# Order of the first loads, and of the work behind them, in a fused state-space and feed-forward kernel

## The chip, the cores and the metric

The kernel runs on one core of one Trainium2 chip. The metric is the device time in microseconds (us). The kernel before takes 155.22 us, the median of three runs; its profiled execution has a span of 152.3 us.

TensorE multiplies matrices and writes the results to the eight banks of PSUM. VectorE, ScalarE and GpSimd do the other arithmetic. Loads are issued from the queues of SyncE and of ScalarE and run on 16 DMA engines that all queues share.

## The reference

For an input x of 2048 rows and 448 columns, two results are computed and mixed row by row with a gate. One is a diagonal complex recurrence (a state-space layer), the other a feed-forward layer:

```python
g  = sigmoid((x * gate_w).sum(-1, keepdims=True))

dt      = exp(log_dt)
Lam_bar = exp(dt * Lam)                       # Lam complex, 448 values
B_bar   = ((Lam_bar - 1.0) / Lam)[:, None] * Bmat
Bu      = einsum("bld,pd->blp", x + 0j, B_bar)
for t in range(L):
    h = Lam_bar[None, :] * h + Bu[:, t, :]
y  = 2.0 * einsum("blp,dp->bld", hseq, Cmat).real + x * Dskip

b  = silu(x @ w1) @ w2                        # w1: 448 x 1792, w2: 1792 x 448
out = g * y + (1 - g) * b
```

## The kernel before

Rows of x are taken in pairs: 1024 pairs, "even" and "odd" rows. The recurrence is run over pairs, so it has 1024 steps; its input is B applied to the odd row plus B scaled by `Lam_bar` applied to the even row. Complex rotation is taken out with tables of sines and cosines, so that the recurrence becomes a real scan on VectorE.

The kernel keeps a list of operations for each engine in program order, and puts a semaphore wait ahead of an operation where it reads or writes what another engine or a load has still to finish. An operation can be several matmuls; its waits stand before the first of them. Within an engine the order of the program is the order of execution.

The loads at the head (`ld` is a plain load, `ldt` a transposing load on SyncE's queue; the first argument of `ld` is the queue that issues):

```python
        for i in range(4):                     # first half of even x, untransposed
            T.dma("act" if i % 2 else "sp", lambda e, i=i: e.dma_start(XH[:, i, :], x0[:, i, :]), writes=COK[i:i + 1])
        ld_w("sp", 0)                          # W1, rows 0 to 127, columns 0 to 767
        for i, (eng, v) in enumerate((("sp", A_log_dt), ("sp", A_Lambda_re), ("act", A_Lambda_im), ("act", A_Dskip))):
            ld(eng, R[i:i + 1, 0:D], row(v), f"R{i}", gR if i < 2 else gR2)
        ld_w("act", 1)
        ld_w("sp", 2)
        ld("act", W1E[0:64, 3, :], B_w1[384:448, :], "W1Ea")
        ld("act", W1E[64:128, 3, :], B_w1[384:448, :], "W1Ez")
        ld("sp", W1E[:, 0:3, FA:], B_w1[0:384, FA:]..., "W1Ed")          # W1, the other columns
        T.op("act", lambda e: e.activation(JK[:, 0, 0:1], HP[:, :], AF.Exp), ...)
        ld("sp", BB[:, 0:6:2, D:], A_B_re[0:384, :]..., "Bre", gB)
        ld("sp", BB[:, 1:6:2, D:], A_B_im[0:384, :]..., "Bim", gB)
        ldt(XT[:, 0:4, 512:1024], x2[512:1024, 0:512], "XTe1")           # second half of even x
        ...                                    # four small loads: B's last 64 rows, into Y3
        for h in range(2):                     # odd x
            ldt(XT[:, 4:7, h * 512:(h + 1) * 512], x2[h * 512:(h + 1) * 512, 512:896], f"XTo{h}")
```

The start of the computation: the first half of even x is transposed on TensorE and copied to SBUF; the first feed-forward pass over six blocks of 128 columns of W1 runs row block by row block; after its first row block (the `yield`) four tiny matmuls turn the parameter rows `R` into columns in PSUM bank 7, from where `PV` is copied.

```python
        for j in range(4):
            T.op("dve", lambda e, j=j: e.tensor_copy(XT[:, j, 0:512], xp[j]), ...)
        T.op("dve", lambda e: e.tensor_copy(XR[64:128, 0:512], xp[3][0:64, :]), reads=["ps7"], writes=["XR0a"])
        T.op("dve", lambda e: e.tensor_copy(XR[0:64, 0:512], xp[3][64:128, :]), reads=["ps7"], writes=["XR0b"])
        rd()                                   # VectorE: copies 64 columns inside R
        first = ffn1_first()
        next(first)
        T.op("pe", mm_cols, reads=["R0", "R1", "R2", "R3", "Rd", "ID"], writes=["ps7"])
        first = next(first)
        T.op("dve", ...)                       # PV <- bank 7
        ...                                    # some 30 tiny operations on PV: dt, mag, sn, cs, lr, li, ...

        def ffn1_first():
            banks = [nxt() for _ in range(NFA)]
            for j in range(4):
                for fb, bank in enumerate(banks):
                    T.op("pe", ... one matmul ..., reads=[f"W1Ej{j}" if j < 3 else "W1Ea", f"XTe0{j}"], ...)
                if j == 0:
                    yield
            yield list(enumerate(banks))
```

Every later feed-forward pass takes up to four column blocks at once: `whole()` has the three full row blocks, one operation for each column block; `rest()` has the last 64 rows, which run in pairs on the two halves of the array (XR holds those rows in the other half of the partitions), and is one operation for all four:

```python
            def rest():
                def mm(pe):
                    for i, (fb, bank) in enumerate(zip(fbs, banks)):
                        up = (i % 2 == 1) != bool(odd)
                        ...
                        ins = pe.matmul(ps[:, bank, :], W[p, jr, fb * 128:(fb + 1) * 128], x,
                                        start=rest_first, stop=not rest_first)
                    return ins
                T.op("pe", mm, ..., writes=[f"ps{bank}" for bank in banks])
```

Each bank is read by a Silu on ScalarE, which frees it. VectorE then works out phases for the tables (`phases(pt)`, three operations on 1024 elements for each of the four groups of 128 states) and the scaled B (`step_B(pt)`), each tile of which is transposed by a load into `LT` for the input projection on TensorE (`bu`):

```python
        step_B(0)
        phases(0)
        step_B(3)          # needs B's last 64 rows in Y3
        step_B(1)
        phases(3)
        step_B(2)
        phases(1)
        phases(2)
```

On TensorE there follow the rest of the feed-forward pass over the first half of even x, the pass over its second half, the input projection, the second feed-forward products, the same for odd x, the products `k0`, and the output tiles. On VectorE there follow the 16 gate sums, the scans, the scaling of C, and the mixing.

Of the kernel before, what the change touches and what calls it, by code (L numbers as in the profile page):

```python
# [19 lines left out]
D = 448  # L20
# [126 lines left out]
def gated_mix(nc, A_x, A_Lambda_re, A_Lambda_im, A_B_re, A_B_im, A_C_re, A_C_im, A_log_dt,  # L147
              A_Dskip, B_x, B_w1, B_w2, gate_w, out):
    with ExitStack() as ctx:
        E = ctx.enter_context  # L150
        T = Tracker(nc, ctx)

        def sb(name, shape, dtype):
            return E(nc.sbuf_tensor(name, list(shape), dtype))
# [4 lines left out]
        XT = sb("XT", [128, 7, NK], BF16)  # L159
# [3 lines left out]
        BB = sb("BB", [128, 7, 2 * D], BF16)  # L163
# [9 lines left out]
        XR = sb("XR", [128, NK], BF16)  # L173
# [29 lines left out]
        ps = E(nc.psum_tensor("ps", [128, 8, 512], F32))  # L203
# [3 lines left out]
        def ld(eng, dst, src, key, group=None):  # L207
            return T.dma(eng, lambda e: e.dma_start(dst, src), writes=[key], group=group)  # L208
# [18 lines left out]
        gR, gR2, gB = T.group(), T.group(), T.group()  # L227
# [19 lines left out]
        ld("act", W1E[0:64, 3, :], B_w1[384:448, :], "W1Ea")  # L247
        ld("act", W1E[64:128, 3, :], B_w1[384:448, :], "W1Ez")
        ld("sp", W1E[:, 0:3, FA:], B_w1[0:384, FA:].rearrange("(j p) f -> p j f", p=128), "W1Ed")
        T.op("act", lambda e: e.activation(JK[:, 0, 0:1], HP[:, :], AF.Exp), reads=["HP"], writes=["JK0"])  # L250
        ld("sp", BB[:, 0:6:2, D:], A_B_re[0:384, :].rearrange("(t p) d -> p t d", p=128), "Bre", gB)
        ld("sp", BB[:, 1:6:2, D:], A_B_im[0:384, :].rearrange("(t p) d -> p t d", p=128), "Bim", gB)
# [5 lines left out]
        for h in range(2):  # L258
# [11 lines left out]
             writes=["IOTA"])  # L270
# [9 lines left out]
        def nxt():  # L280
            n_bank[0] += 1
            return BANKS[(n_bank[0] - 1) % len(BANKS)]

        def ffn1_mm(c, fbs, rest_first):


            odd, h = c // 2, c % 2
            hs = slice(h * 512, (h + 1) * 512)
            W, w0, x0, jr = (W1O, 1, 4, 0) if odd else (W1E, 0, 0, 3)
            banks = [nxt() for _ in fbs]  # L290
            xk = XE[h] + [f"XTo{h}"] if odd else XE[h]

            def whole():
                for fb, bank in zip(fbs, banks):
                    def mm(pe, fb=fb, bank=bank):
                        ins = None
                        for j in range(3):
                            ins = pe.matmul(ps[:, bank, :], W[:, w0 + j, fb * 128:(fb + 1) * 128],  # L298
                                            XT[:, x0 + j, hs], start=(j == 0 and not rest_first),
                                            stop=(j == 2 and rest_first))  # L300
                        return ins
                    wk = ["W1Ob"] if odd else ["W1Ej0", "W1Ej1", "W1Ej2"] if fb < NFA else ["W1Ed"]
                    T.op("pe", mm, reads=wk + xk, writes=[f"ps{bank}"])

            def rest():
                def mm(pe):
                    ins = None
                    for i, (fb, bank) in enumerate(zip(fbs, banks)):
                        up = (i % 2 == 1) != bool(odd)
                        p = slice(64, 128) if up else slice(0, 64)  # L310
                        x = XT[p, 3, hs] if up == bool(odd) else XR[p, hs]
                        ins = pe.matmul(ps[:, bank, :], W[p, jr, fb * 128:(fb + 1) * 128], x,  # L312
                                        start=rest_first, stop=not rest_first)
                    return ins
                wk = ["W1Oa", "W1Oz"] if odd else ["W1Ea", "W1Ez"]
                T.op("pe", mm, reads=wk + xk + [f"XR{h}a", f"XR{h}b"],
                     writes=[f"ps{bank}" for bank in banks])

            for part in (rest, whole) if rest_first else (whole, rest):
                part()  # L320
            return list(zip(fbs, banks))
# [5 lines that stand above are left out]
                p = slice(0, 128 if j < 3 else 64)  # L327

                for fb, bank in enumerate(banks):
                    T.op("pe", lambda pe, fb=fb, bank=bank, j=j, p=p: pe.matmul(  # L330
                        ps[:, bank, :], W1E[p, j, fb * 128:(fb + 1) * 128], XT[p, j, 0:512],
                        start=(j == 0), stop=(j == 3)),
                        reads=[f"W1Ej{j}" if j < 3 else "W1Ea", f"XTe0{j}"], writes=[f"ps{bank}"])
                if j == 0:
                    yield
            yield list(enumerate(banks))

        def ffn1_act(c, fb, bank):
# [12 lines left out]
        def rd():  # L351
            T.op("dve", lambda e: e.tensor_copy(R[:, D:512], R[:, 384:448]), reads=["R0", "R1", "R2", "R3"],
                 writes=["Rd"])
# [17 lines left out]
        for i in range(2):  # L371
            for j in range(4):
                def mm(pe, j=j, i=i):
                    ins = None
                    for k in (2 * i, 2 * i + 1):
                        ins = pe.transpose(xp[j][:, k * 128:(k + 1) * 128], XH[:, k, j * 128:(j + 1) * 128], ID[:, :])
                    return ins
                T.op("pe", mm, reads=COK[2 * i:2 * i + 2] + ["ID"], writes=[f"ps{4 + j}"])
        for j in range(4):
            T.op("dve", lambda e, j=j: e.tensor_copy(XT[:, j, 0:512], xp[j]), reads=[f"ps{4 + j}"], writes=[f"XTe0{j}"])  # L380
        T.op("dve", lambda e: e.tensor_copy(XR[64:128, 0:512], xp[3][0:64, :]), reads=["ps7"], writes=["XR0a"])
        T.op("dve", lambda e: e.tensor_copy(XR[0:64, 0:512], xp[3][64:128, :]), reads=["ps7"], writes=["XR0b"])
        rd()
        first = ffn1_first()
        next(first)
        T.op("pe", mm_cols, reads=["R0", "R1", "R2", "R3", "Rd", "ID"], writes=["ps7"])
# [3 lines left out]
            reads=["ps7"], writes=["PV"])  # L390
# [12 lines left out]
        def c1(n, pt):  # L403
            i = pc(n)
            return P[:, i, pt:pt + 1]
# [32 lines left out]
        for o, up, low in (("ba", "lr", "li"), ("bb", "nli", "lr")):  # L438
# [10 lines left out]
            reads=["f2"] + SGN, writes=["f2s"])  # L449
# [47 lines left out]
        def step_B(pt):  # L497
            if pt < 3:
                lincombs([(BB[:, m, 0:D], f"BB{m}", BB[:, m, D:], c1("lr", pt), BB[:, m ^ 1, D:],
                           c1("li" if m % 2 else "nli", pt), B_RAW + ["lr", "li", "nli"])  # L500
                          for m in (2 * pt, 2 * pt + 1)])
            else:
                T.op("dve", lambda e: e.tensor_copy(BB[0:64, 6, D:], Y3[0:64, 0, :]), reads=["By00"],
                     writes=["Bx3a"])
                T.op("dve", lambda e: e.tensor_copy(BB[64:128, 6, D:], Y3[64:128, 1, :]), reads=["By11"],
                     writes=["Bx3b"])
                lincombs([(BB[:, 6, 0:D], "BB6", Y3[:, 0, :], c1("ba", 3), Y3[:, 1, :], c1("bb", 3),
                           B3 + ["ba", "bb"])])
# [350 lines left out]
def bass_gated_mix__ssm_conv_s5__dense_activation_silu__prompt_kernel(nc, *args):  # L859
    gated_mix(nc, *args)  # L860
# [28 lines left out]
```

## Time and profile before

The busy time of each engine in the span of 152.3 us:

| engine | busy us | share of the span | instructions |
|---|---|---|---|
| TensorE, matmuls | 146.5 | 96% | 756 |
| VectorE | 120.4 | 79% | 234 |
| ScalarE | 63.5 | 42% | 111 |
| GpSimd | 4.9 | 3% | 15 |

The loads of the head, with the time at which each was issued and the time from there to its landing:

| load | queue | KB | issued, us | to landing, us |
|---|---|---|---|---|
| W1 row block 1 (first columns) | ScalarE | 192 | 2.58 | 5.2 |
| W1 other columns | SyncE | 768 | 3.24 | 8.8 |
| B real | SyncE | 336 | 3.71 | 9.1 |
| B imaginary | SyncE | 336 | 4.38 | 9.5 |
| second half of even x, transposed | SyncE | 512 | 5.47 | 14.5 |
| all of x for the gate | ScalarE | 1792 | 12.85 | 10.4 |

In the lines of the profile PE is TensorE, DVE is VectorE, ACT is ScalarE and SPq is SyncE's queue. A name such as L298 is a line of the kernel. TensorE's matmuls are pipelined, so its busy share says little of how near it is to its peak; what counts is where it stood idle and for what. A wait for several things is put down to the one that came last by the profile, which is not always the true one.

### The profile page before, as it was taken

The page shows a single profiled execution, that of the slowest core. Times are in us where ns is not written, and L with a number is a line of the kernel's source. Part 1 is how long each engine was busy: PE and PEld are TensorE (multiplying, and loading weights), DVE is VectorE, ACT ScalarE, POOL GpSimd, SP SyncE. Part 2 cuts the span into 40 slices and gives each one's busy share as a digit, 9 for nine tenths or more (in the row PEclk, how much of TensorE's full clock was granted, in tenths as well). Part 3 has the DMA queues.
Part 4 walks back from the last instruction along what each step waited for, and adds up shares of the span by engine and source line. Part 5 has one row for each costly group of instructions (what it writes and reads, how often), then busy time and mean ns, then how long its engine had stood idle before and what let it go on. Part 6 is the DMA issues. An engine that isn't in the chain of part 4 may idle for free.

```text
span 152.3 us, 2020 instructions
## 1 busy us (share of the span) xinstructions
PE 146.5 (96%) x756; PEld 69.9 (46%) x756; DVE 120.4 (79%) x234; ACT 63.5 (42%) x111; POOL 4.9 (3%) x15
## 2 busy tenths in 40 slices
PE   6989979999999999999999999999999999999993
PEld 2533334344444455433455443555555555555552
DVE  1566809999999999999999999999997017876333
ACT  0359358999977502364731194612234110000000
POOL 7000030000000000000000000000000000000000
PEclk9999999999999999999999999999999999999999
DMA  4999999989737600049537000000000001111221
GB/s 144 258 275 288 306 276 181 201 169 225 246 73 211 269 2 0 0 101 125 129 53 238 0 0 4 0 2 0 0 0 4 0 0 60 60 60 60 89 96 60
DMA packets 26401, 16.25 MB, mean 107 GB/s; under 512 B 17940, under 2 KB 25112, under 8 KB 26392
## 3 DMA queue, kind: packets, MB, share of 16 engines
q1 hardware_dynamic: 24468, 13.15, 35.9%
q10 hardware_dynamic: 1924, 2.98, 6.6%
q8 instruction: 6, 0.10, 0.3%
q14 instruction: 3, 0.02, 0.0%
HBM read 9.93 MB, written 1.84 MB: 77 GB/s over the span
## 4 chain that ended last, share of the span: by engine, by line
PE 85%; DMA 10%; SPq 3%; issue 0%; DVE 0%
PE ps L634 28%; PE ps L298 18%; PE ps L750 14%; PE ps L650 14%; DMA XT<-in_A_x_dram 10%; PE ps L754 4%; PE ps L665 4%; PE ps L312 3%; SPq L208 2%; SPq L237 1%; DVE OT L761 0%; PE ps L667 0%
## 5 line engine op out<-in xcount | busy, mean ns | idle before, releaser
L634 PE MATMUL ps<-W,AT 128*128 128x448 bf16 x224 | 43.0, 352 | 0.0
L340 ACT ACTIVATE AT<-ps 128x512 bf16<-128x512 f32 x56 | 28.9, 624 | 14.6 <-PE ps L312 14.2
L634 PEld LDWEIGHTS ps<-W,AT 128*128 128x128 bf16 x224 | 21.8, 98 | 20.6 <-issue 0.2
L639 ACT ACTIVATE LT<-ps,GT 128x448 bf16<-128x448 f32 x16 | 9.9, 633 | 31.1 <-PE ps L634 24.1
L650 PE MATMUL ps<-XT,LT 128*128 128x512 bf16 x98 | 21.3, 379 | 0.0
L298 PE MATMUL ps<-XT,W1O 128*128 128x512 bf16 x84 | 19.1, 379 | 0.0
L298 PE MATMUL ps<-XT,W1E 128*128 128x512 bf16 x66 | 14.9, 380 | 1.0 <-DMA XT<-in_A_x_dram 1.0
L686 DVE TENSOR_TENSOR_SCAN G<-P,Q 128x1024 f32<-128x1024 f32 x7 | 15.7, 2276 | 0.0
L650 PEld LDWEIGHTS ps<-XT,LT 128*128 128x128 bf16 x98 | 9.6, 98 | 11.5
L761 DVE SCALAR_TENSOR_TENSOR OT<-ps,GT,LT 128x448 bf16<-128x448 f32 x8 | 5.5, 684 | 11.6 <-PE ps L754 11.5
L298 PEld LDWEIGHTS ps<-XT,W1O 128*128 128x128 bf16 x84 | 7.9, 98 | 10.6 <-issue 1.7
L750 PE MATMUL ps<-CO,HS 128*128 128x448 bf16 (+1 forms) x63 | 11.9, 332 | 0.0
L750 PE MATMUL ps<-CE,HS 128*128 128x448 bf16 x56 | 11.9, 352 | 0.0
L298 PEld LDWEIGHTS ps<-XT,W1E 128*128 128x128 bf16 x66 | 6.1, 98 | 9.6 <-DMA XT<-in_A_x_dram 1.5
L654 ACT ACTIVATE HS<-ps 128x512 bf16<-128x512 f32 x14 | 8.5, 648 | 3.2 <-PE ps L650 2.6
L761 DVE SCALAR_TENSOR_TENSOR OT<-ps,GT,W1E 128x448 bf16<-128x448 f32 (+1 forms) x9 | 5.7, 632 | 4.7 <-PE ps L750 4.7
L601 DVE SCALAR_TENSOR_TENSOR JK<-W1O,GWB 128x448 bf16<-128x448 bf16 x16 | 8.8, 618 | 0.0
L683 DVE TENSOR_TENSOR Q<-G,SIN 128x1024 bf16<-128x1024 f32 x7 | 8.5, 1217 | 0.0
L683 DVE TENSOR_TENSOR Q<-G,COS 128x1024 bf16<-128x1024 f32 x7 | 8.5, 1209 | 0.0
L750 PEld LDWEIGHTS ps<-CO,HS 128*128 128x128 bf16 x63 | 6.1, 98 | 4.7
L750 PEld LDWEIGHTS ps<-CE,HS 128*128 128x128 bf16 x56 | 5.5, 98 | 5.1
L754 PE MATMUL ps<-KT,XT 128*128 128x448 bf16 x32 | 7.4, 352 | 0.0
(84 smaller groups left out, 145.2 us busy)
## 6 DMA issues: line engine op xcount, KB each, us to landing
W1O<-in_A_x_dram ACTq DMA_DIRECT2D x1, 1792.0 KB, 10.4
W<-in_B_w_dram SPq DMA_DIRECT2D x1, 1568.0 KB, 7.3
out_dram<-OT SPq DMA_DIRECT2D x7, 224.0 KB, 1.9
W1O<-in_B_w_dram SPq DMA_DIRECT2D x1, 1344.0 KB, 7.4
W1E<-in_A_x_dram SPq DMA_DIRECT2D x1, 896.0 KB, 6.1
W1E<-in_B_w_dram SPq DMA_DIRECT2D x1, 768.0 KB, 8.8
W1E<-in_B_w_dram ACTq DMA_DIRECT2D x2, 224.0 KB, 7.1
W1O<-in_B_w_dram SPq DMA_DIRECT2D x2, 224.0 KB, 3.5
```

The lines of the kernel that those rows point to most:

```text
L298: ins = pe.matmul(ps[:, bank, :], W[:, w0 + j, fb * 128:(fb + 1) * 128], XT[:, x0 + j, hs], start=(j == 0 and not rest_first), stop=(j == ...
L340: T.op("act", lambda e: e.activation(a[:, fb, :], ps[:, bank, :], AF.Silu), reads=[f"ps{bank}"], writes=[f"AT{c % 2}_{fb}"])
L601: T.op("dve", lambda e, t=t: e.scalar_tensor_tensor(JK[:, t % 2, :], XN[:, t * D:(t + 1) * D], 1.0, GWB[:, :], ALU.mult, ALU.mult, accum_o ...
L634: ins = pe.matmul(ps[:, bank, 0:D], a[:, fb, q * 128:(q + 1) * 128], W2[:, fb, :], start=(fb == 0), stop=(fb == NFB - 1))
L639: T.op("act", lambda e: e.activation(bs(tile), ps[:, bank, 0:D], AF.Copy, scale=GT[:, 2, tile:tile + 1]), reads=[f"ps{bank}", "GT2"], writ ...
L650: ins = pe.matmul(ps[:, bank, :], LT[:, m, j, :], XT[:, j, h * 512:(h + 1) * 512], start=(j == 0), stop=(j == 6))
L654: T.op("act", lambda e: e.activation(HS[:, m, 8 + h * 512:8 + (h + 1) * 512], ps[:, bank, :], AF.Copy), reads=[f"ps{bank}", f"F{pt}"], wri ...
L683: T.op("dve", lambda e: e.tensor_tensor(o, a, b, op), reads=reads, writes=writes)
L686: T.op("dve", lambda e: e.tensor_tensor_scan(G[:, c, :], rb, Q1[:, c, :], 0.0, ALU.mult, ALU.add), reads=[f"Q1{c}", "rr"], writes=[f"G{c}"])
L750: ins = pe.matmul(ps[:, b, c], HS[:, m, o0:o0 + 128], C[:, m, c], start=(m == 0), stop=(odd == 1 and m == 6))
L754: ins = pe.matmul(ps[:, b, c], XT[:, j, t0:t0 + 128], KT[:, j, c], start=False, stop=(j == 3))
L761: T.op("dve", lambda e, b=b, c=c: e.scalar_tensor_tensor(o[:, odd * D:(odd + 1) * D][:, c], ps[:, b, c], GT[:, 1, tile:tile + 1], (BG[:, k ...
```

## The change

It moves work and adds none. The two big loads of B go from SyncE's queue to ScalarE's, so that the transposing load of the second half of even x stands before B and not behind it. VectorE does two phase groups before it needs B. The four matmuls for the parameter columns go from the end of the first row block to the middle of the second, and the copy inside R goes ahead of the two XR copies. The operation of the last 64 rows is cut into one operation for each pair, so that a pair waits only for its own two banks and releases them by itself.

```diff
         ld("sp", W1E[:, 0:3, FA:], B_w1[0:384, FA:]..., "W1Ed")
+        ld("act", BB[:, 0:6:2, D:], A_B_re[0:384, :]..., "Bre", gB)
+        ld("act", BB[:, 1:6:2, D:], A_B_im[0:384, :]..., "Bim", gB)
         T.op("act", lambda e: e.activation(JK[:, 0, 0:1], HP[:, :], AF.Exp), reads=["HP"], writes=["JK0"])
-        ld("sp", BB[:, 0:6:2, D:], A_B_re[0:384, :]..., "Bre", gB)
-        ld("sp", BB[:, 1:6:2, D:], A_B_im[0:384, :]..., "Bim", gB)
         ldt(XT[:, 0:4, 512:1024], x2[512:1024, 0:512], "XTe1")
@@ rest()
-                def mm(pe):
-                    ins = None
-                    for i, (fb, bank) in enumerate(zip(fbs, banks)):
-                        ...
-                    return ins
-                T.op("pe", mm, reads=wk + xk + [f"XR{h}a", f"XR{h}b"],
-                     writes=[f"ps{bank}" for bank in banks])
+                for i in range(0, len(fbs), 2):
+                    def mm(pe, i=i):
+                        ins = None
+                        for fb, bank, up in zip(fbs[i:i + 2], banks[i:i + 2], (bool(odd), not odd)):
+                            ...
+                        return ins
+                    T.op("pe", mm, reads=wk + xk + [f"XR{h}a", f"XR{h}b"],
+                         writes=[f"ps{bank}" for bank in banks[i:i + 2]])
@@ ffn1_first()
-                if j == 0:
-                    yield
+                    if j == 1 and fb == 2:
+                        yield
@@
+        rd()
         T.op("dve", lambda e: e.tensor_copy(XR[64:128, 0:512], xp[3][0:64, :]), reads=["ps7"], writes=["XR0a"])
         T.op("dve", lambda e: e.tensor_copy(XR[0:64, 0:512], xp[3][64:128, :]), reads=["ps7"], writes=["XR0b"])
-        rd()
@@
+        phases(0)
+        phases(3)
         step_B(0)
-        phases(0)
         step_B(3)
         step_B(1)
-        phases(3)
         step_B(2)
         phases(1)
         phases(2)
```

More of the change, by code (lines that the diff above doesn't have):

```diff
@@ L249, in gated_mix @@
         ld("sp", W1E[:, 0:3, FA:], B_w1[0:384, FA:].rearrange("(j p) f -> p j f", p=128), "W1Ed")
+        ld("act", BB[:, 0:6:2, D:], A_B_re[0:384, :].rearrange("(t p) d -> p t d", p=128), "Bre", gB)
+        ld("act", BB[:, 1:6:2, D:], A_B_im[0:384, :].rearrange("(t p) d -> p t d", p=128), "Bim", gB)
         T.op("act", lambda e: e.activation(JK[:, 0, 0:1], HP[:, :], AF.Exp), reads=["HP"], writes=["JK0"])
-        ld("sp", BB[:, 0:6:2, D:], A_B_re[0:384, :].rearrange("(t p) d -> p t d", p=128), "Bre", gB)
-        ld("sp", BB[:, 1:6:2, D:], A_B_im[0:384, :].rearrange("(t p) d -> p t d", p=128), "Bim", gB)
         ldt(XT[:, 0:4, 512:1024], x2[512:1024, 0:512], "XTe1")
@@ L305, in rest @@
             def rest():
-                def mm(pe):
-                    ins = None
-                    for i, (fb, bank) in enumerate(zip(fbs, banks)):
[L309 to L313, printed above, removed]
-                    return ins
-                wk = ["W1Oa", "W1Oz"] if odd else ["W1Ea", "W1Ez"]
-                T.op("pe", mm, reads=wk + xk + [f"XR{h}a", f"XR{h}b"],
-                     writes=[f"ps{bank}" for bank in banks])
+                wk = ["W1Oa", "W1Oz"] if odd else ["W1Ea", "W1Ez"]
+                for i in range(0, len(fbs), 2):
+                    def mm(pe, i=i):
+                        ins = None
+                        for fb, bank, up in zip(fbs[i:i + 2], banks[i:i + 2], (bool(odd), not odd)):
+                            p = slice(64, 128) if up else slice(0, 64)
+                            x = XT[p, 3, hs] if up == bool(odd) else XR[p, hs]
+                            ins = pe.matmul(ps[:, bank, :], W[p, jr, fb * 128:(fb + 1) * 128], x,
+                                            start=rest_first, stop=not rest_first)
+                        return ins
+                    T.op("pe", mm, reads=wk + xk + [f"XR{h}a", f"XR{h}b"],
+                         writes=[f"ps{bank}" for bank in banks[i:i + 2]])
             for part in (rest, whole) if rest_first else (whole, rest):
```

## The prediction

> **What bounds the kernel now.** I read the tenths of the page first, for where TensorE is not full. Each digit is the busy tenth of a slice of 3.8 us.
>
> ```profile
> PE   6989979999999999999999999999999999999993
> ACT  0359358999977502364731194612234110000000
> PEclk9999999999999999999999999999999999999999
> DMA  4999999989737600049537000000000001111221
> ```
>
> TensorE is at nine tenths from the seventh slice to the last, at full granted clock. What is not full lies in the first six slices, some 23 us, in which the DMA engines are saturated. Next, the waits of TensorE alone (engine and line, what it waited for, total us, times, longest):
>
> ```profile
> PE ps L365 <- DVE SG L224: 1.3, 1, 1.3
> PE ps L298 <- DMA XT<-in_A_x_dram: 1.0, 1, 1.0
> PE ps L358 <- DVE R L352: 0.5, 1, 0.5
> PE ps L312 <- DVE P L410: 0.2, 1, 0.2
> ```
>
> These and a wait of 0.2 us at 6.10 us are all of them. The first is the start-up, which the change leaves alone. The other three add to 1.01 + 0.52 + 0.19 = 1.72 us, and that is nearly all that any reordering of the head can win. Third, the chain that ended last (start, length, what):
>
> ```profile
> 5.47 14.51 DMA XT<-in_A_x_dram
> 19.99 0.05 issue
> 20.03 2.76 PE ps L298 x12
> ...
> 52.36 10.59 PE ps L634 x56
> ...
> 149.75 0.45 DVE OT L761
> ```
>
> The end is set by the transposing load of the second half of even x (issued at 5.47 us, landed at 19.99), and from 20.03 us on by TensorE alone, matmul after matmul, to 149.7. So a microsecond won before 20 us is a microsecond at the end, as long as nothing new stops TensorE later. Last, the same chain further up, in SyncE's queue (start, length, issue), which shows why that load is late:
>
> ```profile
> 3.24 0.43 SPq L208
> ...
> 3.71 0.62 SPq L208
> ...
> 4.38 1.05 SPq L208
> ```
>
> The first is the issue of the 768 KB of W1's remaining columns; the next two are B's real and imaginary parts, 336 KB each, and only then comes the transpose. B landed at 3.71 + 9.1 = 12.8 and 4.38 + 9.5 = 13.9 us, W1's columns at 3.24 + 8.8 = 12.0.
>
> **What the Trainium skill says.** *DMA: Bandwidth & Descriptors*, section "Queues, rings and completion order": SP and ACT each own one row of rings on the same 16 DMA engines, each engine serves a ring in order, and round-robins between rows at packet granularity. The same page, "Issuing engines are not separate DMA queues", says that issuing from two engines saves only issue time. The trace agrees: in the windows of one microsecond the mean DMA share is 0.97 to 1.28 nearly everywhere from 3 to 20 us, with both queues in use. So moving B to ScalarE's queue makes no bandwidth; what it does is take B out of the ring *ahead of* the transpose and set it *beside* it. *PSUM — Partial Sum Buffer*, "PSUM bank collisions raise a hardware error", has PSUM guarded by bank: a matmul must wait for its bank's reader. The 0.19 us wait is such a wait; the releaser named, VectorE's parameter line, is not a reader of those banks. The reader is the second Silu: three Silus start at 11.36 us and take 1.57 together, so two are done near 12.4, and the matmul starts at 12.59. *Perfetto Trace Analysis*, "DMA Instruction — HWDGE (DVE, Sync)", says that the profiled length of an issue ends when the sequencer is free, not when data has moved. The trace agrees: the transpose's issue is 8.05 us long and its data lands 6.5 us after that.
>
> **The change, part by part.**
>
> *Second half of even x ahead of B, and B on ScalarE.* No byte is added or removed. The transpose can be issued at 3.71 instead of 5.47 us, 0.62 + 1.05 us of issue plus gaps sooner: 1.76 us. In its ring it stands behind W1's columns (12.0 us) instead of behind B (13.9 us): 1.9 us sooner. Between 13.9 and 19.99 it shared the engines with ScalarE's 112 KB broadcast and 1,792 KB load of x (issued 12.45 and 12.85); now it shares them with B, then with those. If sharing with B is like sharing with x, it takes the same 6.1 us and lands near 12.0 + 6.1 = 18.1; by the issue, at 19.99 - 1.76 = 18.2. I take 18.2 to 18.7, since B's rows may also slow W1's columns a little.
>
> *B's price on ScalarE.* Two issues of 0.6 to 1.05 us put the first table load from 4.20 to about 5.9; 1.28 for it and 0.20 for the dummy Exp end at 7.4. The first real Exp started at 8.56, so this is hidden with over 1 us to spare.
>
> *Parameter columns mid-pass, R's copy first.* The four tiny matmuls need R's copy and also PSUM bank 7, which the two XR copies read. Those three DVE operations end at 7.77 + 0.16 = 7.93 in whatever order, so R's copy in front frees nothing by itself. But three more matmuls (18 of this pass took 4.16 us with the last one's tail, so about 0.22 each and 0.65 for three) now stand between. They need W1's second row block, which landed at 2.58 + 5.2 = 7.78. TensorE is done with the first six at 8.08 - 0.52 = 7.56, so 0.52 of idle becomes about 0.22: 0.3 us won. The price: the columns start near 7.78 + 0.65 = 8.43 instead of 8.08, and the whole parameter chain is 0.35 us later. ScalarE's last Sin then ends at 11.35 instead of 11.00. The Silu behind it waited 0.36 us for TensorE until 11.36 anyway, so it starts where it did.
>
> *One operation per pair.* TensorE is at the half-height matmuls at 12.40 - 0.3 = 12.10. The first pair writes banks 6 and 7, long free, and needs the half row block that landed near 3.6 + 8.3 = 11.9; it runs at once, 0.22 us. The second pair still waits for the second Silu, to about 12.6. The full-height matmuls start at 12.8 instead of 13.05: of the 0.3 won before, about 0.25 is left, because this point is held by ScalarE, not by TensorE.
>
> *Rotation phases ahead of the B scaling.* VectorE's parameters end near 12.93 + 0.35 = 13.3. Two phase groups of 0.75 + 0.69 + 1.23 = 2.67 bring it to 18.7 us, and B is then needed at 18.7 instead of 13.9: this is what pays for B landing late. The 4.02 us for which VectorE stood idle for B's last 64 rows (until 22.56) are filled, so VectorE is some 4 us ahead at the gate (36.05 before, about 32 now). It does not set the end: the first k0 matmul at 111.27 used data ready at 105.4, the first y tile at 122.29 used data ready at 112.3. So this brings slack, no time.
>
> *The sum.* TensorE reaches the wait for x at 20.03 - 1.01 - 0.25 = 18.77 us. If x has landed (18.2 to 18.7), it goes on at once, and 20.03 - 18.77 = 1.26 us are won; if x lands at 19.2, 0.8. I put the mean at 1.1 us. After that nothing new should stop it: the first input projection, at 31.04 before and about 29.9 now, needs the first transposed B tile, which landed at 23.88 + 4.9 = 28.8. That queue also moves up by about 1.8 us, as its transposes stand behind the x loads and B is scaled by 20.8. 155.22 - 1.1 = 154.1.
>
> **The rivals.** *(a) The load is not ahead at all.* If packets alternate between rows and B is now a rival all along, the transpose could land as late as before, and 0 to 0.3 us are won: 155.0. For it: total bytes ahead of 20 us are the same. Against: in before, the transpose also had a rival in x's 1,792 KB. *(b) W1's columns become the wait.* B in ScalarE's ring now competes with the columns needed at 12.8; they landed at 12.04, a margin of 0.8. If B takes half of the engines once ScalarE's own weights are in, they could be a microsecond later, which costs 0.3 us and pushes the transpose too: 155.2. *(c) ScalarE's queue is blocked by the issue of B*, as SyncE's was for 8.05 us by the transpose: Exp, Silu and all behind would be late by up to 3 us: 157 to 158. Against: ScalarE's two issues at 12.45 and 12.85, in the middle of that transpose, took 0.36 and 0.44 us. *(d) B lands after 18.7*, the transposed B tiles come late and stop the input projection. It would need B later than about 22: 155 to 156. *(e) Everything fits and the parameter chain isn't late:* all 1.7 us are won: 153.5.
>
> **Range and chances.** The ceiling of 1.72 us puts the floor at 153.5, and with 0.2 of scatter 153.3. Rivals (a) and (b) end at about 155.2. Range 153.3 to 155.3. Faster by 2% would be 152.1, beyond all idle there is: 0.02. Slower by 2% would be 158.3, only (c) or a new long stall: 0.03.
>
> **What would show it.** Right: the transpose is issued near 3.7 and landed before 18.8, no or under 0.3 us of TensorE wait on x; the wait of 0.52 on R gone, one of about 0.2 on weights in its place; phases before B on VectorE without a wait at 18.7; TensorE without a gap after 20 us. Wrong: x landing near 20, a wait on W1's columns near 12.8, ScalarE's first table load after 7 us, or any gap between 29 and 33 us.

## The result, and the profile after

The changed kernel took 153.14 us (median of four runs, 152.85 to 153.78) against 155.16 us for the kernel before, the median of four runs of which one took 259.82 us and the others 155.01 to 155.22. (That one is also among the three runs behind the 155.22 us given at the head.) Without it the ratio is 0.9879, 95% interval 0.9838 to 0.9919. The 153.14 us are 0.16 us below the range predicted. The traced run of the changed kernel has a span of 152.1 us, and it is the slowest of the four (153.78 us).

The busy tenths of the changed kernel, in slices of 3.8 us:

```profile
PE   6797999999999999999999999999999999999993
DMA  4999999989999100485280000000000001111221
```

All of TensorE that is not full lies in the first four slices, but for the last one. The waits of TensorE in the changed kernel (engine and line, what it waited for, total us, times, longest):

```profile
PE ps L365 <- DVE SG L224: 1.3, 1, 1.3
PE ps L313 <- DMA W1E<-in_B_w_dram: 1.0, 1, 1.0
PE ps L330 <- DMA W1E<-in_B_w_dram: 0.9, 1, 0.9
```

The waits for x, for R and for the second Silu are gone. Two waits on W1 stand in their place: one on its first row block at 6.24 us, one on its last rows at 13.24 us. The chain that ended last goes through a third part of W1, its other columns, which came just behind those rows (start, length, what):

```profile
3.24 10.62 DMA W1E<-in_B_w_dram
13.86 0.05 issue
13.91 5.35 PE ps L298 x24
```

W1's other columns, issued at the same 3.24 us as before, landed at 13.86 instead of 12.04. The transposing loads in SyncE's queue (start, length of the issue, what), and the first user of the second half of even x on GpSimd:

```profile
3.71 9.15 SPq L211 DMA_TRANSPOSE XT<-in_A_x_dram  x1
...
15.46 11.73 SPq L211 DMA_TRANSPOSE XT<-in_A_x_dram  x2
27.30 9.27 SPq L211 DMA_TRANSPOSE LT<-BB  x7
```

```profile
18.03 1.14 POOL L218 COPY XR<-XT 64x512 bf16<-64x512 bf16 x1 [13.96 <-DMA XT<-in_A_x_dram]
```

x was issued at 3.71 and used at 18.03 us. But the two transposes of odd x took 11.73 us to issue where they took 7.50, and the transposed B tiles start at 27.30 where they started at 23.88.

**This pair of traces shows only 0.3 us of the 2.0.** Once TensorE is at the input projection (L650), nothing stops it, and the rest takes the same time: the span less the start of L650 is 152.3 - 31.04 = 121.3 us before and 152.1 - 30.74 = 121.4 after (121.2 to 121.4 in every trace of the runs below). So each traced run's time is made ahead of the input projection, and a trace explains the time of the run that it was taken from. The trace of the kernel before is of a run of 154.08 us, not of one of 155.2; that of the changed kernel is of a run of 153.78. That gap had to be settled first.

### The profile page after: what moved, and what is told of

The parts are those of the page before. It is cut to its first block, busy times and chain, and to the rows that moved or that the text cites. A ratio compares the mean times of both kernels' runs of the same rounds, so it can differ in the third digit from the quotient of the medians.

```text
span 152.1 us, 2020 instructions
## 1 busy us (share of the span) xinstructions
PE 146.1 (96%) x756; PEld 69.2 (46%) x756; DVE 121.1 (80%) x234; ACT 64.1 (42%) x111; POOL 5.4 (4%) x15
## 4 chain that ended last, share of the span: by engine, by line
PE 89%; DMA 7%; SPq 1%; DVE 0%; issue 0%
PE ps L634 28%; PE ps L298 22%; PE ps L750 14%; PE ps L650 14%; DMA W1E<-in_B_w_dram 7%; PE ps L754 4%; PE ps L313 4%; PE ps L665 4%; SPq L208 1%; SPq L237 1%; DVE OT L761 0%; PE ps L667 0%
## 5 line engine op out<-in xcount | busy, mean ns | idle before, releaser
L340 ACT ACTIVATE AT<-ps 128x512 bf16<-128x512 f32 x56 | 29.2, 620 | 13.0 <-PE ps L313 12.5
L650 PE MATMUL ps<-XT,LT 128*128 128x512 bf16 x98 | 21.3, 379 | 0.0
L298 PE MATMUL ps<-XT,W1O 128*128 128x512 bf16 x84 | 19.1, 379 | 0.0
L650 PEld LDWEIGHTS ps<-XT,LT 128*128 128x128 bf16 x98 | 9.6, 98 | 11.5
```

The source lines that it names most:

```text
L340: T.op("act", lambda e: e.activation(a[:, fb, :], ps[:, bank, :], AF.Silu), reads=[f"ps{bank}"], writes=[f"AT{c % 2}_{fb}"])
L650: ins = pe.matmul(ps[:, bank, :], LT[:, m, j, :], XT[:, j, h * 512:(h + 1) * 512], start=(j == 0), stop=(j == 6))
```

## The experiments

Each run is timed against the kernel before on the same chip. The ratio is not the quotient of the two medians: it is worked out from the fast runs alone, those within 1.5% of the fastest of their kernel. The theories named in the expectations: *theory 1*, the trace of before lacks about 1 us of waiting for x that its usual run has, and the load order is worth 2 us; *theory 2*, the TensorE parts (columns mid-pass, pairs) carry half of the gain; *theory 3*, the change is worth about 1 us, and the other microsecond belongs to the first comparison.

| run | median us | before beside it (runs) | ratio, 95% interval |
|---|---|---|---|
| kernel before again | 154.00 | 154.09 (58) | 1.0011 (0.9982 to 1.0041) |
| B's loads moved, nothing else | 153.21 | 154.09 | 0.9956 (0.9932 to 0.9981) |
| all but B's loads | 153.85 | 154.09 | 0.9987 (0.9958 to 1.0016) |
| B on SyncE behind x | 153.23 | 154.09 | 0.9961 (0.9939 to 0.9982) |
| changed kernel, second comparison | 153.15 | 154.20 (43) | 0.9956 (0.9936 to 0.9977) |
| phases put back | 153.18 | 154.20 | 0.9944 (0.9925 to 0.9962) |
| first block split | 160.04 | 154.20 | 1.0370 (1.0315 to 1.0424) |
| split, B behind x, gate load later | 158.85 | 154.20 | 1.0254 (1.0199 to 1.0309) |
| split, x issued after the half rows | 154.29 | 154.39 (68) | 0.9980 (0.9954 to 1.0006) |
| the same, gate load later | 154.96 | 154.39 | 0.9976 (0.9950 to 1.0003) |
| changed kernel, gate load later | 153.27 | 154.39 | 0.9932 (0.9909 to 0.9954) |
| changed kernel, third comparison | 153.26 | 154.39 | 0.9947 (0.9919 to 0.9975) |
| kernel before, gate load later | 152.99 | 154.18 (11) | 0.9921 (0.9902 to 0.9940) |
| split, parameter rows on SyncE | 153.21 | 154.18 | 0.9938 (0.9914 to 0.9963) |
| the same, gate load later | 152.96 | 154.34 (19) | 0.9927 (0.9900 to 0.9953) |
| gate load later, TensorE parts, B as before | 152.67 | 154.34 | 0.9915 (0.9886 to 0.9945) |
| the same once more | 152.91 | 154.35 (26) | 0.9901 (0.9885 to 0.9916) |
| changed kernel, fourth comparison | 153.40 | 154.35 | 0.9938 (0.9916 to 0.9960) |

### What is the kernel before's usual time?

The unchanged kernel before:

> The kernel before, unchanged, to see its trace once more. Theory 1 (the recorded trace of before took 154.08 us where its median is 155.2, so that trace misses about 1.1 us of waiting that a usual run has, most likely for the second half of even x): ratio 1.000; the trace, if its run takes about 155.2, shows a wait of TensorE for x of about 2 us instead of 1.0, with x landing near 21. Theory 2 (the trace is typical, and the extra gain comes from TensorE's own order): ratio 1.000 and again a wait of about 1.0 us for x.

It took 154.00 us (median of 14 runs); its trace is of a run of 154.39. Three lines of TensorE's timeline in it (start, length, instruction, idle before and releaser):

```profile
6.85 1.47 PE L330 MATMUL ps<-XT,W1E 128*128 128x512 bf16 x6 [0.82 <-DMA W1E<-in_B_w_dram]
20.31 2.76 PE L298 MATMUL ps<-XT,W1E 128*128 128x512 bf16 x12 [1.10 <-DMA XT<-in_A_x_dram]
31.32 1.89 PE L650 MATMUL ps<-XT,LT 128*128 128x512 bf16 x8
```

The wait for x is 1.10 us, not 2: theory 1 falls. What differs from the first trace is the first feed-forward matmul, at 6.85 instead of 6.10 us, held by W1's first block, which is the first load behind the first half of x and which the change doesn't touch. It landed at 6.80 us here and at 5.60 in the first trace.

The changed kernel, three times more against many runs of the kernel before:

> The changed kernel, unchanged, against the kernel before on one chip with many runs of each. In the call before, the kernel before had a median of 154.09 us over 58 runs, not 155.16 over three. Theory 3 (the change is worth about 1 us, as the trace says, and the other 1 us of the first comparison lies in when the very first loads land on a given chip): ratio 0.992 to 0.995. Theory 1 (the change is worth 2 us everywhere): ratio 0.986 to 0.989.

> The changed kernel against the kernel before once more, if possible on a third chip. If the change is worth about 1 us: ratio 0.992 to 0.997, with the kernel before near 154.1. If the 155.2 of the first three runs belongs to a chip or a session: a kernel before near 155 here would show it, and the ratio would be near 0.988.

> The changed kernel on the same chip: ratio 0.994 to 0.997, near 153.2 us, with the kernel before near 154.2, if the three comparisons of about 1.1 us are the rule; ratio near 0.988 if the first one is.

The differences of the medians are 1.05, 1.13 and 0.95 us, on two chips; the ratios, taken of about 154.3 us, give 0.7, 0.8 and 1.0. The kernel before has a median of 154.00 to 154.39 in every set of runs in the table, on four chips. Theory 3 holds for these: the change is worth 0.7 to 1.1 us. It is not worth that in every run: of the 239 runs of the kernel before in this table, 29 took under 153.4 us, as little as the changed kernel usually takes (17 of the 29 on one chip). No trace of such a run was kept. The first comparison's interval ends at 0.9919, below the ratios of the other three (0.9956, 0.9947, 0.9938); its kernel before has three ordinary runs, 155.01 to 155.22 us. Why all three were a microsecond above every later median was not found: 12 of the 239 later runs took 155.0 us or more, and no trace of such a run exists. It stays open whether it was the chip or something else.

The changed kernel's trace in the second comparison (153.25 us):

```profile
7.04 2.12 PE L330 MATMUL ps<-XT,W1E 128*128 128x512 bf16 x9 [0.91 <-DVE R L352]
13.37 5.35 PE L298 MATMUL ps<-XT,W1E 128*128 128x512 bf16 x24
30.21 10.09 PE L650 MATMUL ps<-XT,LT 128*128 128x512 bf16 x46
```

There is no wait at 13 us here: the wait on W1's last rows that stands in the first trace is not in every run. The rest is in the first line. (Its releaser is named as VectorE's copy of R, which this matmul doesn't read; the weight load in front of it waited 1.2 us for W1.) It helps to measure from the first feed-forward matmul to L650:

| trace | first matmul | L650 | between |
|---|---|---|---|
| before, first trace | 6.10 | 31.04 | 24.94 |
| before again | 6.85 | 31.32 | 24.47 |
| changed, first trace | 6.24 | 30.74 | 24.50 |
| changed, second comparison | 7.04 | 30.21 | 23.17 |
| changed, third comparison | 6.92 | 30.17 | 23.25 |
| changed, fourth comparison | 6.35 | 29.59 | 23.24 |

Three of four traces of the changed kernel have no idle of TensorE in that stretch that the profile lists; the fourth has the 1.02 us at 13.24. The start itself scatters: by 0.75 us between the two traces of the kernel before, by 0.80 in the four of the changed kernel, mostly with the landing of W1's first block (5.6 to 7.0 us). This scatter is nearly as large as the change's gain, and it can hide it in a comparison of few runs.

The wait of 0.52 us on R belongs to this scatter too. In the first trace TensorE started early, at 6.10, and stood for R until 8.08. In the second it started at 6.85, was done with its first six matmuls at about 8.3, and the wait on R is gone, without any change: the late start used it up. So the wait on R and the wait on W1's first block are in part the same time, and what the columns mid-pass can win is smaller in a run whose first block is late.

### Which part carries the gain?

B's two loads moved to ScalarE, so that x is ahead, and nothing else:

```diff
+        ld("act", BB[:, 0:6:2, D:], ..., "Bre", gB)
+        ld("act", BB[:, 1:6:2, D:], ..., "Bim", gB)
         T.op("act", lambda e: e.activation(JK[:, 0, 0:1], HP[:, :], AF.Exp), ...)
-        ld("sp", BB[:, 0:6:2, D:], ..., "Bre", gB)
-        ld("sp", BB[:, 1:6:2, D:], ..., "Bim", gB)
         ldt(XT[:, 0:4, 512:1024], ...)
```

> The kernel before with the two B loads on ScalarE's queue, and so x ahead, and nothing else of the change. Theory 1 (the order of the loads carries the gain): ratio 0.988 to 0.992, 153.3 to 153.9 us, no wait for x left, a wait for W1's columns near 13 us instead. Theory 2 (the pair operations and the parameter columns carry half): ratio about 0.994, 154.2 us.

The changed kernel with those lines put back:

> The changed kernel with B back on SyncE's queue ahead of x: columns mid-pass, pairs and phases only. Theory 1: ratio 0.997 to 1.000, 154.7 to 155.1 us, since TensorE then waits for x all the longer. Theory 2: ratio about 0.994, 154.2 us.

The move alone has the ratio of the whole change in the second comparison (0.9956); the rest without it has 0.9987, an interval that holds 1 and leaves out the 0.994 of theory 2. Theory 2 falls as it was put. The move's own 0.9956 is also above the 0.988 to 0.992 of theory 1: the 2 us did not come. A share of a few tenths for the TensorE parts is not excluded by these intervals. The trace of the move alone (TensorE's waits, and x's first user):

```profile
PE ps L365 <- DVE SG L224: 1.3, 1, 1.3
PE ps L358 <- DVE R L352: 0.5, 1, 0.5
PE ps L312 <- DVE P L410: 0.2, 1, 0.2
```

```profile
15.93 0.69 POOL L218 COPY XR<-XT 64x512 bf16<-64x512 bf16 x1 [11.87 <-DMA XT<-in_A_x_dram]
```

x is there at 15.9 us, and its wait is gone; the two small waits that the TensorE parts aim at are still there. In the trace of those parts without the move, x still lands at 20.3, and TensorE waits for it:

```profile
20.32 2.76 PE L298 MATMUL ps<-XT,W1E 128*128 128x512 bf16 x12 [0.87 <-DMA XT<-in_A_x_dram]
```

These matmuls start when x has landed, as they did at 20.03 and 20.31 in the two traces of the kernel before. What the parts won ahead of that point could not count.

The phases back behind the scaling of B (`step_B(0)`, `phases(0)`, `step_B(3)`, `step_B(1)`, `phases(3)`, ... as before):

> The changed kernel with the phases where they were, behind the scaling of B. If the phases pay for B landing late only on VectorE, which has slack: same time as the changed kernel within 0.2 us, VectorE waiting some 2 to 3 us for B near 14. If the transposed B tiles or the tables depend on it: 0.5 us or more slower than the changed kernel, with a wait of TensorE at the input projection.

```profile
14.43 0.82 DVE L490 TENSOR_SCALAR TMP<-BB,P 128x448 f32<-128x448 bf16 x2 [1.02 <-DMA BB<-in_A_B_im_dram]
```

VectorE waits 1.02 us for B (less than the 2 to 3 expected), and the time is the same, 153.18 against 153.15 us. The order on VectorE brings slack and no time.

### B beside W1, or behind x?

B on SyncE's queue behind x, everything else as changed:

```diff
-        ld("act", BB[:, 0:6:2, D:], ..., "Bre", gB)
-        ld("act", BB[:, 1:6:2, D:], ..., "Bim", gB)
         ldt(XT[:, 0:4, 512:1024], x2[512:1024, 0:512], "XTe1")
+        ld("sp", BB[:, 0:6:2, D:], ..., "Bre", gB)
+        ld("sp", BB[:, 1:6:2, D:], ..., "Bim", gB)
```

> The changed kernel with B on SyncE's queue, but behind the transposing load of x. If B beside W1's columns in the other ring is what makes TensorE wait 1.02 us for them in the trace of the changed kernel: that wait gone, ratio 0.982 to 0.985, 152.4 to 152.8 us, with B landing near 17. If W1's columns are late for another reason, or B now comes too late for the transposed B tiles: ratio 0.987 or more, 153.1 us and up.

153.23 us: neither faster nor slower than the changed kernel. x's first user starts at 13.87 us, B's second part landed at 19.1 (near 17 was expected), and there is no wait on W1's last rows. But as that wait is missing from three of the changed kernel's own four traces, this run does not show that B beside W1 makes it. Against it speaks the trace of all but B's loads: there B was behind W1's columns in SyncE's own queue, and the columns still landed at 13.16 us. Why they are a microsecond or more late in some traces stays open.

### What made x late?

In the kernel before, B was left ahead of x, and only the 1,792 KB load of x for the gate, on the other queue, was moved:

```diff
-        load_xn()
         run(ffn1(0, NFA))
+        load_xn()
```

> The kernel before, with B ahead of x as it was, and only the 1,792 KB load of x for the gate moved behind the first feed-forward pass. If B ahead in the ring is the cause: x lands 0 to 1 us sooner, the ratio is 0.997 to 1.000. If sharing with that load is the cause: x lands 2 us or more sooner, its wait of 1 us is gone, ratio near 0.994, the same as the change brings.

152.99 us (six runs), ratio 0.9921. SyncE's transposing loads of x, x's first user, and the longest of TensorE's waits, of which none is for x any more:

```profile
5.29 8.29 SPq L211 DMA_TRANSPOSE XT<-in_A_x_dram  x1
...
16.16 3.63 SPq L211 DMA_TRANSPOSE XT<-in_A_x_dram  x2
```

```profile
16.20 0.86 POOL L218 COPY XR<-XT 64x512 bf16<-64x512 bf16 x1 [12.14 <-DMA XT<-in_A_x_dram]
```

```profile
PE ps L330 <- DMA W1E<-in_B_w_dram: 1.3, 1, 1.3
```

x was issued nearly as late as before (5.29 us against 5.47), behind B as before, and was there at 16.2 instead of 20.0. The gate's load, issued at 12.85 in the middle of x's transfer, had cost it nearly 4 us. The transposes of odd x also fall from 7.50 to 3.63 us of issue. So one moved line without the change does what the change does, and either removes the wait: the wait came from the sharing with the gate's load as much as from the place in the queue.

The same line moved in the changed kernel:

> The changed kernel with the 1,792 KB load of x for the gate issued after the first feed-forward pass, nothing else. SyncE's two transposes of odd x, 11.5 us of issue in the changed kernel, should take about 4, and the first transposed B tile land 5 us sooner. If the input projection is at its limit there in usual runs: 0.2 to 0.4 us under the changed kernel. If TensorE sets the time alone: the same within 0.15 us.

The transposes of odd x took 3.64 us and the transposed B tiles started at 20.34 instead of 27.30, yet the time is 153.27 us beside 153.26 for the changed kernel: x no longer held anything, so there was nothing to win. The margin of 0.3 us that the changed kernel's first trace left at the projection (27.30 + 3.1 = 30.4 for the first tile, 30.74 for its user) was not yet a limit.

### Can the wait on the first block go?

W1's first row block as two halves, one on each queue:

```diff
-        ld_w("sp", 0)
+        gJ0 = T.group()
+        ld("sp", W1E[0:64, 0, 0:FA], B_w1[0:64, 0:FA], "W1Ej0", gJ0)
+        ld("act", W1E[64:128, 0, 0:FA], B_w1[64:128, 0:FA], "W1Ej0b", gJ0)
```

> The changed kernel with W1's first row block loaded as two halves of 64 rows, one from each queue. If the scatter between runs and the wait of 0.8 to 0.9 us at the first feed-forward matmul come from that block sharing the engines with the blocks behind it: the wait under 0.3 us, median 0.3 to 0.6 us under the changed kernel, and a smaller scatter. If the block is late for its latency and not for its share: no difference.

> B on SyncE's queue behind x, W1's first block split over both queues, and the 1,792 KB load of x for the gate issued after the first feed-forward pass instead of in it. If SyncE's transposes of odd x were blocked by that load: they take 8 us instead of 10, and the first transposed B tile lands over 2 us before TensorE needs it, not 0.1. Time 152.4 to 152.8 us on a chip where the kernel before takes 154.1; if nothing but the first block matters, the same as the run with the split alone.

160.04 and 158.85 us: far slower. Neither expectation had that. The first of the two in TensorE's timeline, and in windows of 2 us (busy us of TensorE, weight loads, VectorE, ScalarE, GpSimd, each with its count; granted clock; DMA share; GB/s):

```profile
6.09 2.10 PE L332 MATMUL ps<-XT,W1E 128*128 128x512 bf16 x9 [0.27 <-DVE XT L382]
...
13.37 1.47 PE L332 MATMUL ps<-XT,W1E 64*128 64x512 bf16 x6 [2.94 <-DMA W1E<-in_B_w_dram]
17.32 0.61 PE L315 MATMUL ps<-XT,W1E 64*128 64x512 bf16 x1 [2.48 <-DMA W1E<-in_B_w_dram]
...
18.28 7.38 PE L300 MATMUL ps<-XT,W1E 128*128 128x512 bf16 x24
```

```profile
14.00:16.00 2.00, 0.83 (x4) 0.19 (x2) 1.93 (x3) 2.00 (x5) 0.00 (x0) 0.90 1.11 128
16.00:18.00 2.00, 0.69 (x4) 0.13 (x4) 1.93 (x4) 0.84 (x2) 0.00 (x0) 0.50 1.20 209
18.00:20.00 2.00, 2.00 (x7) 0.62 (x6) 0.86 (x1) 0.22 (x1) 0.00 (x0) 0.50 1.26 198
```

The wait on the first block did fall: what is left there is 0.27 us, put down to VectorE's copy. But ScalarE issued its last two W1 loads (the 64 rows, twice) 0.6 to 0.7 us later, the second at 4.21, just behind the transposing load of x at 4.17 us, and it landed 13.1 us after that, at 17.3; in the changed kernel's four traces it was issued near 3.55, about 0.15 us ahead of the transposing load, and landed at 12.2 to 13.2. TensorE stood for 2.94 and 2.48 us, and then its granted clock was 0.50 from 16 to 22 us: the 24 matmuls took 7.38 instead of 5.35 us. In each of the four traces where TensorE stood for 1.9 us or more at one place (these two, and those of the next two runs) the clock fell to half for a time; in the other traces, with waits of up to 1.4 us, its mean stayed at 0.998 or above. That it fell because TensorE had stood is what this suggests; no run tests it.

Was it the halves or the order behind them? B's real part was put ahead of the transposing load on SyncE's queue, so that this load is issued later:

> The split of W1's first block again, but with B's real part on SyncE's queue ahead of the transposing load, so that this load is issued after ScalarE's last 64 rows of W1 and not with them. Theory A (in the run with the split alone, ScalarE's weights were issued 0.6 us later, beside and behind the transposing load, and that is why they landed 3 to 4 us later): the rows land near 12 again, no clock below 0.98, 152.5 to 153.0 us. Theory B (the halves themselves are slow): 157 us and up again.

> The two runs before together. If both hold: 152.3 to 152.8 us; if theory B holds: 157 us and up.

154.29 and 154.96 us: most of the 6 us is back, but not all, and theory A's own figures did not come. The single runs spread from 153.38 to 156.70 us in the first and from 153.35 to 159.09 in the second. The traces are of runs of 156.70 and 156.31 us. In that of the first the last rows were issued at 4.28, half a microsecond ahead of the transposing load at 4.77, and still landed at 14.56 (near 12 was expected); TensorE waited for them:

```profile
PE ps L315 <- DMA W1E<-in_B_w_dram: 2.7, 1, 2.7
```

Then ScalarE's two parameter rows went to SyncE's queue. This puts ScalarE's W1 loads further ahead, of the transposing load and also of W1's other columns, the 768 KB that SyncE issues just in front of it:

```diff
-        for i, (eng, v) in enumerate((("sp", A_log_dt), ("sp", A_Lambda_re), ("act", A_Lambda_im), ("act", A_Dskip))):
+        for i, (eng, v) in enumerate((("sp", A_log_dt), ("sp", A_Lambda_re), ("sp", A_Lambda_im), ("sp", A_Dskip))):
```

> The changed kernel with W1's first block as two halves on the two queues, and with ScalarE's two parameter rows on SyncE's queue, so that ScalarE's last 64 rows of W1 are issued no later than in the changed kernel and well before the transposing load. If their place relative to that load is what counts: they land by 12.5 us, the wait on the first block is under 0.5 us, 152.3 to 152.9 us. If the halves harm in another way: 154 us or more.

> The run with the split first block and the parameter rows on SyncE's queue (153.21 us), with the gate's load of x moved behind the first feed-forward pass. If the waits left there (0.58 us on the first block, 0.33 us on W1's columns) and x near its limit share the engines with that load: 152.5 to 152.9 us. If not: 153.2 us as before.

With the halves still split, 153.21 and 152.96 us, both above their forecasts. In the first of them ScalarE's last rows are issued at 3.75 us, W1's other columns at 4.16 and the transposing load at 4.63; the rows land at 10.51 (by 12.5 was expected), the wait on the first block is 0.58 us (under 0.5 was expected), and x's user starts at 18.62. So the halves do no harm, and theory B falls. The order of issue does: with the same halves, 160.04, 154.29 and 153.21 us. Theory A holds in that, but not in naming the neighbour: the last step moved the rows ahead of W1's columns as well as further ahead of the transposing load, and no run separates the two. The gain from the split itself is not resolved (0.9938 against 0.9938 to 0.9956 for the changed kernel).

### The gate's load later, with parts of the change

Columns mid-pass, pairs and phases from the change, B left on SyncE's queue ahead of x, and the gate's load moved:

> The changed kernel with B back on SyncE's queue ahead of x, and the gate's load of x moved behind the first feed-forward pass: the columns mid-pass, the pairs and the phases on top of the run that moved that load alone. If the parts add up: the waits on R and on the second Silu gone, 0.3 to 0.5 us under 153.0. If W1's first block sets the floor in any order: 153.0 within 0.15 us.

> The gate's load later, columns mid-pass, pairs and phases, B on SyncE's queue ahead of x. If it is really better than the change: ratio 0.990 to 0.993, and 0.3 us or more under the changed kernel beside it. If the run of 152.67 us was six lucky runs: 153.1 us.

152.67 and 152.91 us. Side by side with the changed kernel on one chip, it is 0.9901 (0.9885 to 0.9916) to 0.9938 (0.9916 to 0.9960), 0.49 us between the medians; the intervals just touch, so that it is likely, and not shown beyond doubt, that it is faster than the changed kernel. That it is faster than the kernel before with the gate's load moved and nothing else (0.9921, another chip) is not resolved. Its trace from the first of the two comparisons (152.43 us):

```profile
PE ps L365 <- DVE SG L224: 1.3, 1, 1.3
PE ps L298 <- issue: 0.5, 3, 0.2
PE ps L330 <- DMA W1E<-in_B_w_dram: 0.4, 1, 0.4
```

No wait for x, R or a Silu is left; what remains is the start-up and W1's first block. (The 0.5 us put down to "issue" goes with eight matmul records that are missing from this trace, 748 of 756.)

## Why the prediction was wrong, and where it was right

**The step that failed is the last line of the sum, "155.22 - 1.1 = 154.1", and with it the floor of the range, "The ceiling of 1.72 us puts the floor at 153.5".** All waits in the sum were read from a trace of a run of 154.08 us, and then taken off 155.22 us, the median of three other runs (155.10, 155.22 and the one of 259.82). The term that was mis-sized is the 155.22: the kernel before measured 154.00 to 154.39 in every later set of runs. 154.08 - 1.1 = 153.0 would have been the consistent figure, with a floor of 154.08 - 1.72 = 152.4, and the changed kernel's medians are 153.14, 153.15, 153.26 and 153.40. The gain of 1.1 us was about right: the three later comparisons have 0.95 to 1.13 us between the medians, 0.7 to 1.0 by the ratios. In the first one it was 2.0 us, more than the three waits of the sum, and what its kernel before lost there is open.

The mechanism, that x ahead of B ends the wait for x, is what the move of B's loads alone showed. That the forecast gain fits is in part luck, as its steps show:

- *The order of the loads.* x was issued at 3.71 as forecast and landed at 17.98 us in the first trace (forecast 18.2 to 18.7), but at 16.56, 16.72 and 15.94 in the other three. TensorE did not wait for it in any. The working behind it, "12.0 + 6.1", took 6.1 us for a property of the transfer. It was mostly the gate's load sharing the engines: with that load away, x landed at 16.2 with B still ahead of it, 2.3 us behind B and not 6.1. In the first trace two errors made up for each other: W1's columns landed at 13.86 and not at 12.0, and x came 4.1 us behind them. Rival (a), that sharing would keep x as late as before, did not come, but sharing weighed far more than I gave it.
- *B's price on ScalarE.* The first table load started at 5.95 us (forecast 5.9) and was hidden. Rival (c) did not happen.
- *Parameter columns mid-pass.* The 0.52 us wait on R is gone and the columns started at 8.53 us in the first trace (forecast 8.43). Not foreseen: the first matmul itself waited 0.88 us for W1's first block, 0.91 to 1.36 in the other traces of the changed kernel, and 0.82 in the second trace of the kernel before. I had seen 0.23 us in one trace and taken it for fixed; a later start takes away most of what this part wins.
- *Pairs.* Forecast: the first pair runs at once and the second waits for a Silu. In the first trace all four waited for W1's last rows: rival (b), with W1's columns 1.8 us late where I had given it a microsecond. In the other three traces of the changed kernel no such wait is seen.
- *Phases ahead of B.* VectorE went from the phases to B at 18.62 without a wait (forecast 18.7), and was at the gate at 32.48 (forecast 32). It brought no time, as said; putting them back showed that.
- *"That queue also moves up by about 1.8 us".* Wrong in sign: the transposed B tiles started at 27.30, 26.89, 25.93 and 25.17 us in the changed kernel's traces, 1.3 to 3.4 us later than the 23.88 before. The gate's load, still under way until 24.8 to 27.1 us (23.3 before), stretched the transposes of odd x; with it away, the tiles started at 20.34. In the first trace this came within 0.3 us of costing time.
- *The ceiling.* The reading that nothing after 20 us stops TensorE held in every trace that was read: span less start of L650 stayed near 121.3 us. No version won more than the 1.72 us; the best won 1.3 and 1.5 us by its ratios.

## What to carry to other kernels

A trace belongs to the run that it was taken from: take the savings that it shows off that run's time, not off a median of other runs, and when the head of a kernel is bound by loads, take several traces of before, as the landing of one early load can scatter by as much as the change is worth, and a short wait behind it may be gone in the next run. When a load is late, look for what is issued *during* it on the other queue before reordering what is ahead of it; here one moved line did as much as the whole change. And what a kernel needs soon is best issued well ahead of the big loads, on either queue: here 0.9 us ahead of the transposing load, and ahead of W1's columns, was enough, and half a microsecond ahead of the one and behind the other was not.

## What was not expected of the hardware

ScalarE's last 64 rows of W1, 224 KB, took 13.1 us to land when they were issued 0.04 us after a transposing load on the other queue, 10.3 us when it was half a microsecond before one, 8.6 to 9.6 us at 0.15 us before one in the changed kernel, and 6.8 us at 0.9 us before one and also before W1's columns. So the distance to the transposing load alone does not order them; what was issued ahead of them differs too. While the transposing load was under way in the split run, from 14 to 16 us, the DMA share was 1.11 but only 128 GB/s were moved, against 0.92 and 282 GB/s from 3.96 to 7.92 us in the same run: a full share is not full bandwidth. The same two transposes of odd x took 3.5 to 4.7 us to issue in the seven traces where the ordinary load of 1,792 KB was issued only after they had begun, and 7.5 to 15.0 us in all others, where it was already under way.
